# A delta-rule attention and slot router on one core: four edits to loads, solution weights, transposes and the shares of the inverse

## The chip, the cores and the metric

The kernel runs on 1 core of one Trainium2 chip. The metric is the device time of one execution in microseconds (us), lower is better. Eight executions of the kernel before the change took 373.21 to 382.68 us, with a median of 375.94 us. The profile in this document is of one execution that took 374.93 us.

The engines are named as the profile names them: PE is the matrix engine (PEld its weight loads), DVE the vector engine, ACT the scalar engine, POOL the general-purpose engine, SP the engine that here only issues DMAs. An ending q (SPq, ACTq) is the engine's instruction queue. Each engine runs its instructions strictly in the order in which they were written to it, and waits at an instruction whose inputs or whose target buffer are not ready, with everything behind it.

## The reference

Two blocks one after the other: a delta rule over 768 positions for 4 batches of 8 heads (head size 48), and a soft mixture of experts with 32 slots.

```python
def _attn_ref(q, k, v, beta):                 # (4, 8, 768, 48), beta (4, 8, 768)
    k_n = k / (np.linalg.norm(k, axis=-1, keepdims=True) + 1e-06)
    for t in range(S):
        kt, vt, bt = (k_n[:, :, t], v[:, :, t], beta[:, :, t, None])
        y[:, :, t] = np.einsum('bhd,bhde->bhe', q[:, :, t], state)
        v_old = np.einsum('bhde,bhd->bhe', state, kt)
        state = state + bt[:, :, :, None] * np.einsum('bhd,bhe->bhde', kt, vt - v_old)
...
def _moe_ref(x, phi, w1, w2):                 # x (3072, 384), 8 experts, F = 1024
    logits = x @ phi
    d = np.exp(logits - logits.max(0, keepdims=True))
    d /= d.sum(0, keepdims=True) + 1e-09
    slot_input = d.T @ x
...
        h = np.maximum(slot_input[e] @ w1[e], 0.0)
        slot_out[e] = h @ w2[e]
...
    c = np.exp(logits - logits.max(1, keepdims=True))
    c /= c.sum(1, keepdims=True) + 1e-09
    return (c @ slot_out).astype(np.float32)
```

## The kernel before

**Chunks and groups.** The 768 positions are cut into 24 chunks `x` of 32 positions. Four chunks make a group: group `n` is chunks 4n to 4n+3, and `c` is the place of a chunk in its group. A chunk covers all 4 batches and 8 heads at once. Within a chunk the recurrence is solved as a triangular system, so each chunk needs the inverse of a 32x32 triangular matrix for every batch and head. The inverses of a whole group are computed together on DVE, one group ahead.

**The recurrence of a chunk** (`chunk`, L392, called from the loop at L711) is a chain over four engines: `rest` (L411) multiplies the state with the keys on PE (L407) and DVE subtracts that from the scaled values into `R` (L414); `solve` (L417) multiplies `R` with the inverse `Tb` on PE (L421) and ACT copies the result to `U` (L424); `update` (L429) adds U times K to the state in `psS` on PE (L434) and ACT copies the new state to SBUF in two pieces (L441); the next chunk's `rest` needs that state. `read` and `outputs` (L426, L446) make the output `Y` beside it.

**The inverse of a group** (`invert`, L229): `spread` (L251) transposes the products of keys `GQ` into `lb` on DVE (L254) and takes the squared norms `ssq`; `root` (L263) is a logarithm and an exponential on ACT (L264, L265); `norms` (L267) is a row of ten DVE instructions that gives `gm`, scales `lb` (L281) and makes `nT`, by which POOL scales the values of that group (`scale_v`, L368, eight instructions at L371 for a chunk). Then come some 95 steps (L297, L302, L330) on DVE, and `back(0)` and `back(1)` transpose the two halves of the result into `TT` (L362). The first group's inverse runs by itself before the loop. For later groups `plan` (L610) deals the steps out over the chunks of the group before: `EL[c][p]` is a list for place p (0, 1, 2) of chunk c. `share` (L608) gives the share of the steps' weight for each place. `norms` stands at the head of `EL[0][0]`, `back(0)` in `EL[2][2]`, `back(1)` in `EL[3][2]`, and what is left of the steps goes to `EL[3][1]`.

**Weights of a chunk** (`weights`, L374) are made on POOL at the end of the chunk before: four instructions (L379) write `Ab`, and four copies (L385) put the inverse of the chunk from `TT` into `Tb`, each to the 32 partitions of one head, at place `h % 2` of a pair; the other place of the pair stays zero from a memset (L158). Both have three buffers, taken in turn.

**Preparation of later chunks** (`Prep`, L182): keys and queries are transposed on PE (L192), copied to `KQ` on ACT (L201, L208), and multiplied (`products`, L210: PE L221, ACT L225 to `GQ`). In the loop this runs eight chunks ahead (`later`, L704; the first chunks have a list of their own, L700, in which `q2 p2` of chunk 0 stands between `read` and `solve`).

**Router** (`route`, L473): each group's outputs are multiplied with `phi`, and softmax over tokens and slots is spread over the next group's chunks in lists `head`, `act`, `mid`, `vec`, `end`. In chunk c = 0 it ends with the logits (L481) and their copy `lT` (ACT L485); in c = 1 DVE begins with the maxima (L489), ahead of `EL[1][0]`; c = 2 ends with the two copies `dr` (ACT L563); sums of slots (PE L572) are added by DVE to `sacc` (L579 to L583) at c = 0.

**Order of one pass through the loop** (L721 to L771): loads are issued on SP; then `hook("head")`, `EL[c][0]`, `rest`, `read`, `scale_v(x + 2)`, `later(x, 0)`, `hook("act")`, `EL[c][1]`, from group 1 on at c = 3 `spread` of the group after next, `solve`, `turn`, `later(x, 1)`, `hook("mid")`, `hook("vec")`, `EL[c][2]`, `update`, `outputs`, `later(x, 2)`, `hook("end")`, `weights(x + 1)`, and at c = 3 `root` of the group after next. The order is written out by hand here; no scheduler changes it.

**Loads.** Keys, queries and values of a chunk are four DMAs of 48 KB each (L82, one for each h). Nearly all are issued from SP in the order of the program; K2 alone is issued from ACT. Eight completion counters are handed to the DMAs in turn, so an issue waits until the DMA eight before it has landed. Four buffers hold queries: Q4, Q5, Q6 share those of Q1, Q2, Q3.

**Experts** (from L784): the weights of the experts are loaded while the loop ends and after it, products on PE, and the output is written.

Of the kernel before, what the change touches and what calls it, by code (L numbers as in the profile page):

```python
# [8 lines left out]
F32 = mybir.dt.float32  # L9
AX = mybir.AxisListType  # L10
ALU = mybir.AluOpType
ACT = mybir.ActivationFunctionType
# [4 lines left out]
def kernel(  # L17
# [25 lines left out]
    nc = tc.nc  # L43
    P = 128
    B, H, S, D = q.shape
    C = 32
# [4 lines left out]
    U = B * G  # L51
# [15 lines left out]
    wk = att.enter_context(tc.tile_pool(name="wk", bufs=2))  # L67
# [18 lines left out]
    def load_k(cc, eng=nc.sync):  # L86
        load(k, Ks[cc % NK], cc, eng)

    def q_of(cc):

        return Qs[(cc - (LEAD // 2 <= cc < LEAD) * 3) % NQ]

    def load_q(cc, eng=nc.sync):
        load(q, q_of(cc), cc, eng)

    def load_v(cc, eng=nc.sync):
        Vt[cc] = io.tile([P, U, D], F32, name="V", tag="V", bufs=5)
        load(v, Vt[cc], cc, eng)
# [1 line left out]
    load_k(0)  # L100
    load_k(2, nc.scalar)
    load_k(1)
    load_k(3)

    one = cpool.tile([P, 1], F32, name="one")
    nc.vector.memset(one, 1.0)
    nc.scalar.preload_act_table_set("natural_log_exp_and_others")
    load_q(0)
    ident = cpool.tile([P, P], F32, name="ident")
    make_identity(nc, ident)  # L110
    for i in range(NK):
# [12 lines left out]
    own = cpool.tile([P, 2], F32, name="own")  # L124
# [13 lines left out]
            out=phi[g * D:(g + 1) * D],  # L138
            in_=moe_phi[g * 4 * D:(g + 1) * 4 * D].rearrange("(h d) s -> d h s", h=4))

    load_v(0, nc.sync)
    for i in range(4, 7):
        load_k(i)
        load_q(i)
    load_k(7)
# [6 lines left out]
        nc.vector.memset(t, 0.0)  # L152

    NT = 3
    Tb = [wk.tile([P, U, 2, C], F32, name=f"Tb{i}", bufs=1) for i in range(NT)]
    Ab = [wk.tile([P, U, 2, C], F32, name=f"Ab{i}", bufs=1) for i in range(NT)]
    for t in Tb + Ab:
        nc.vector.memset(t, 0.0)  # L158


# [19 lines left out]
    KQ, GQ, TT, nT = {}, {}, {}, {}  # L180
# [187 lines left out]
    def scale_v(cc):  # L368
        n, c = divmod(cc, GC)
        for u in range(U):  # L370
            nc.gpsimd.tensor_scalar(Vt[cc][:, u], Vt[cc][:, u], nT[n][:, c * U + u:c * U + u + 1],  # L371
                                    None, op0=ALU.mult)

    def weights(cc):  # L374
        n, c = divmod(cc, GC)
        for h in range(4):
            r = slice(C * h, C * h + C)

            nc.gpsimd.affine_select(  # L379
                out=Ab[cc % NT][r, :, h % 2, :].rearrange("p (b g) t -> p b g t", g=G),  # L380
                in_=GQ[n][r, c, :, :, 1, :], compare_op=ALU.is_gt, fill=0.0, base=0,
                pattern=[[0, B], [0, G], [1, C]], channel_multiplier=-1)
        for h in range(4):
            r = slice(C * h, C * h + C)
            nc.gpsimd.tensor_copy(Tb[cc % NT][r, :, h % 2, :], TT[n][r, c * U:(c + 1) * U, :])  # L385

# [3 lines left out]
    def chunk(cc, Yn):  # L392
        n, c = divmod(cc, GC)
        kq, K = KQ.pop(cc), Ks[cc % NK]
        at, T = ([t[cc % NT][64 * y:64 * y + 64].rearrange("p u x t -> p u (x t)")
                  for y in range(2)] for t in (Ab, Tb))
        half = [slice(64 * y, 64 * y + 64) for y in range(2)]
        old, new = St[cc % 2], St[1 - cc % 2]
        hs = [slice(C * h, C * h + C) for h in range(4)]
        st = {}  # L400

        ks, qs = (t[:, 0:U * D].rearrange("p (b g d) -> p b g d", g=G, d=D) for t in (psR, psY))

        def state(a, dst):
            for b in range(B):
                for h in range(4):
                    nc.tensor.matmul(dst[hs[h], b].rearrange("p g d -> p (g d)"),  # L407
                                     lhsT=kq[:, b, a, hs[h]], rhs=old[:, h, b, :],
                                     start=(b == 0), stop=False, skip_group_check=True)

        def rest():  # L411
            state(0, ks)
            R = st["R"] = wk.tile([P, U, D], F32, name="R", tag="R", bufs=1)
            nc.vector.tensor_tensor(R, Vt.pop(cc), ks.rearrange("p b g d -> p (b g) d"),  # L414
                                    op=ALU.subtract)

        def solve():  # L417
            pw = psR[:, 0:U * D].rearrange("p (u d) -> p u d", d=D)
            for u in range(U):
                for y in range(2):  # L420
                    nc.tensor.matmul(pw[half[y], u], lhsT=T[y][:, u], rhs=st["R"][half[y], u],  # L421
                                     start=(u == 0), stop=True, skip_group_check=True)
            st["U"] = wk.tile([P, U, D], F32, name="U", tag="U", bufs=1)
            nc.scalar.activation(st["U"], pw, ACT.Copy)  # L424

        def read():  # L426
            state(1, qs)

        def update():  # L429
            if cc == NCH - 1:  # L430
                return
            for b in range(B):
                for h in range(4):
                    nc.tensor.matmul(  # L434
                        psS[0:DP + D, h, b * GD:(b + 1) * GD],
                        lhsT=K[hs[h], b * G:(b + 1) * G].rearrange("p g d -> p (g d)")[:, 0:DP + D],
                        rhs=st["U"][hs[h], b * G:(b + 1) * G].rearrange("p g d -> p (g d)"),
                        start=(cc == 0 and b == 0), stop=True, skip_group_check=True)
            for g in range(G):
                r = slice(DP * g, DP * g + D)  # L440
                nc.scalar.activation(  # L441
                    new[r, :, :, g * D:(g + 1) * D],
                    psS[r, :, 0:B * GD].rearrange("p h (b g e) -> p h b g e", b=B, g=G)[:, :, :, g],
                    ACT.Copy)

        def outputs():  # L446
            for b in range(B):
                for g in range(G):
                    u = b * G + g
                    for y in range(2):  # L450
                        nc.tensor.matmul(qs[half[y], b, g], lhsT=at[y][:, u],  # L451
                                         rhs=st["U"][half[y], u],
                                         start=False, stop=True, skip_group_check=True)
            nc.scalar.activation(Yn[:, c, :, 0:GD], qs.rearrange("p b g d -> p b (g d)"),
                                 ACT.Copy)

        return rest, solve, read, update, outputs
# [137 lines left out]
    def drain(ls):  # L595
        for f in ls:
            f()
# [7 lines left out]


    PLACES = 3
    share = [(0.0, 0.14, 0.15), (0.10, 0.10, 0.10), (0.09, 0.09, 0.08), (0.10, 0.05, 0.0)]  # L608

    def plan(n):  # L610

        f = invert(n)
        at = [[[] for _ in range(PLACES)] for _ in range(GC)]
        at[0][0] += [f["norms"]]
        todo, done, total = f["steps"], 0.0, 0.0
        whole = sum(t[0] for t in todo)
        i = 0
        for c in range(GC):
            for p in range(PLACES):
                total += share[c][p] * whole  # L620
                while i < len(todo) and done + todo[i][0] / 2 < total:
                    done += todo[i][0]
                    at[c][p].append(todo[i][1])
                    i += 1
        at[2][2] += [lambda: f["back"](0)]
        at[3][1] += [t[1] for t in todo[i:]]
        at[3][2] += [lambda: f["back"](1)]
        return f, at
# [15 lines left out]
    f0["norms"]()  # L644
    pre[0].alone(1, 0)
    load_q(7)
    f0["clear"]()
    drain([t[1] for t in f0["steps"]])
    for i in range(2):
        f0["back"](i)  # L650
    pre[0].products(1, 2)
    for cc in range(4, 8):
        pre[cc] = Prep(cc)
        pre[cc].alone(0, 1)
        pre[cc].alone(1, 0)
        if cc > 4:
            pre[cc - 1].products()
    load_q(1)
    load_v(1)
    load_k(8)  # L660
    load_q(2)
    load_q(8)
    load_v(2)
    load_k(9)
    load_q(3)
    load_v(3)
    load_k(10)
    load_k(11)
    pre[7].products()
    pre[1].alone(1, 0)  # L670
    pre[1].products(1, 2)
    scale_v(0)
    weights(0)
    scale_v(1)

    empty = [[[]] * PLACES] * GC
    f, EL = plan(1)
    f["unit"]()
    f["spread"]()
    f["clear"]()  # L680
    f["root"]()
    routing, yT, late = [{}] * (GC + 1), {}, {}


# [19 lines left out]
    def later(x, place):  # L704
        if x in ahead:
            for w in ahead[x][place].split():
                step(int(w[1:]), w[0])
        else:
            step(x + LEAD + (place > 0), "ptu"[place])

    for x in range(NCH):  # L711
        n, c = divmod(x, GC)
# [4 lines left out]
        def hook(name):  # L717
            drain(late.get(name, []) if c == 0 else [])
            drain(routing[c].get(name, []))
# [20 lines left out]
        if x + 2 < NCH:  # L740
            scale_v(x + 2)
        later(x, 0)
        hook("act")
        drain(EL[c][1])
        if follow and x > GC:
# [2 lines left out]
        if x > 0:  # L748

            m, i = divmod(x - 1, GC)  # L750
# [15 lines left out]
        if c == GC - 1:  # L766
            EL = empty
            if follow:
                f, EL = follow
# [116 lines left out]
    for n in range(NG):  # L886
        for b in range(B):
            i = n * B + b
# [37 lines left out]
```

## Time and profile before

| | us |
|---|---|
| this execution | 374.93 |
| its span in the profile | 373.2 |
| first solve (L421, chunk 0) starts | 52.00 |
| R of chunk 4, 8, 12, 16, 20 starts | 94.08, 137.68, 184.03, 225.65, 264.55 |
| R of chunk 23 starts | 286.96 |
| last weights w2 landed | 346.8 |

The rows of the chunks are the starts of DVE's L414, one for each chunk. Between two of them lies the period of a chunk: 8 to 14 us in groups 1 to 4, where DVE also carries the inverse, 7 to 8 us in group 5, where it doesn't. After chunk 23 the chain goes through the last routing, the experts' first products at 306 us and the last loads of w2, and the output.

In a timeline row the columns are: start in us from the span's beginning, duration in us (of the whole run of equal instructions if there are several), engine, line, operation, output and inputs, shapes, number; in brackets the idle time of the engine ahead of it and what released it. In the group rows "x24 | 11.8, 492" means 24 instructions, 11.8 us of busy time, 492 ns for one. The engines' totals and the chain of waits are in the next part, as far as its steps rest on them.

### The profile page before, as it was taken

Reading aid. Unit: us, or ns where it says so; the run is one execution under the profiler, and the core shown is the slowest. Engines: PE = TensorE matmul, PEld = TensorE weight load, DVE = VectorE, ACT = ScalarE, POOL = GpSimd, SP = SyncE. Lnnn points to the kernel's source line nnn. Section 1 sums busy time; section 2 is a strip of 40 time slices with the busy share of each in tenths; the row PEclk is TensorE's granted clock in tenths of the full one; section 3 lists DMA queues with packets and bytes.
Section 4 is the critical chain, followed back from the end, with each engine's and each line's share of the span. In section 5 each row is a group of like instructions: output and inputs, shape, how many; then the busy total and the mean of one; then the engine's idle time right before and its main releaser. Section 6 shows DMA issues by size and latency. Waiting matters only on the chain.

```text
span 373.2 us, 16124 instructions
## 1 busy us (share of the span) xinstructions
PE 287.6 (77%) x6879; PEld 227.5 (61%) x6879; DVE 239.2 (64%) x801; ACT 145.3 (39%) x292; POOL 201.7 (54%) x434
## 2 busy tenths in 40 slices
PE   3667557887877989689788797689988779864784
PEld 2445446775766878578677676578877663311252
DVE  8399999785968979779696988889131220101043
ACT  2443124565334744356444652235455312000032
POOL 8460099993999379970899629994990000000000
PEclk9995659999589998679998998768999969999785
DMA  6555555554433344354101111105001997999058
GB/s 99 92 89 94 81 94 90 89 80 79 80 58 60 63 75 101 84 102 90 35 15 23 25 25 24 23 10 185 4 4 25 407 423 333 356 432 391 4 208 298
DMA packets 85031, 45.24 MB, mean 121 GB/s; under 512 B 79424, under 2 KB 82656, under 8 KB 83040
## 3 DMA queue, kind: packets, MB, share of 16 engines
q1 hardware_dynamic: 83296, 43.86, 43.7%
q8 instruction: 54, 0.88, 1.0%
q0 software_dynamic: 576, 0.15, 0.3%
q10 hardware_dynamic: 1088, 0.20, 0.3%
q14 instruction: 17, 0.14, 0.1%
HBM read 39.47 MB, written 4.72 MB: 118 GB/s over the span
## 4 chain that ended last, share of the span: by engine, by line
PE 47%; DVE 18%; SPq 11%; DMA 11%; ACT 7%; issue 4%; POOL 1%; DVEq 0%; ACTq 0%; POOLq 0%
SPq L82 10%; PE psR L421 7%; PE psS L434 6%; PE pt L572 6%; DMA w2t<-in_moe_w_dram 6%; PE psY L451 5%; PE pt L192 4%; PE pt L469 4%; PE pso L864 3%; DMA Q<-in_q_dram 3%; DVE R L414 3%; DVE tt L302 3%; ACT S L441 3%; DVE prL L297 2%; PE ph L840 2%
## 5 line engine op out<-in xcount | busy, mean ns | idle before, releaser
L371 POOL TENSOR_SCALAR V<-V,nT 128x48 f32<-128x48 f32 x192 | 91.2, 499 | 9.6 <-DMA Q<-in_q_dram 7.4
L385 POOL COPY Tb<-TT 32x256 f32<-32x256 f32 x96 | 43.1, 449 | 63.7 <-DVE TT L362 59.4
L421 PE MATMUL psR<-R,Tb 64*64 64x48 f32 x768 | 30.7, 234 | 32.1 <-DVE R L414 22.3
L379 POOL TENSOR_SCALAR_AFFINE_SELECT Ab<-GQ 32x256 f32<-32x256 f32 x96 | 48.2, 502 | 3.5
L421 PEld LDWEIGHTS psR<-R,Tb 64*64 64x64 f32 x768 | 28.1, 149 | 35.6 <-issue 25.9
L441 ACT ACTIVATE S<-psS 48x768 f32<-48x768 f32 x46 | 37.1, 806 | 27.1 <-PE psS L434 26.9
L221 PE MATMUL pt<-KQ 48*32 48x64 f32 (+1 forms) x1792 | 26.3, 237 | 12.6 <-ACT KQ L208 9.6
L424 ACT ACTIVATE U<-psR 128x384 f32<-128x384 f32 x24 | 11.8, 492 | 59.8 <-PE psR L421 47.4
L221 PEld LDWEIGHTS pt<-KQ 48*32 48x32 f32 x1792 | 21.3, 119 | 18.9 <-ACT KQ L208 11.1
L297 DVE TENSOR_TENSOR prL<-tt,nm 128x256 f32<-128x256 f32 (+7 forms) x96 | 29.7, 314 | 2.8
L297 DVE TENSOR_TENSOR prM<-tt,lb 128x16 f32<-128x16 f32 (+7 forms) x96 | 31.0, 323 | 0.0
L302 DVE TENSOR_TENSOR tt<-tt,prL 128x256 f32<-128x256 f32 (+7 forms) x96 | 30.9, 321 | 0.2
L302 DVE TENSOR_TENSOR nm<-nm,prM 128x16 f32<-128x16 f32 (+7 forms) x96 | 30.6, 319 | 0.0
L451 PE MATMUL psY<-U,Ab 64*64 64x48 f32 x768 | 30.1, 233 | 0.0
L302 DVE TENSOR_TENSOR tt<-tt,prE 128x30 f32<-128x30 f32 (+7 forms) x90 | 29.8, 331 | 0.0
L225 ACT ACTIVATE GQ<-pt 128x256 f32<-128x256 f32 (+1 forms) x56 | 16.7, 351 | 31.4 <-PE pt L221 31.4
L451 PEld LDWEIGHTS psY<-U,Ab 64*64 64x64 f32 x768 | 27.0, 147 | 2.7 <-issue 0.7
L297 DVE TENSOR_TENSOR prE<-tt,lb 128x30 f32<-128x30 f32 (+7 forms) x90 | 28.5, 317 | 0.0
L434 PE MATMUL psS<-U,K 32*112 32x96 f32 x736 | 27.7, 295 | 0.1
L434 PEld LDWEIGHTS psS<-U,K 32*112 32x112 f32 x736 | 23.6, 198 | 4.6 <-issue 2.0
L572 PE MATMUL pt<-Y,dr 64*64 64x97 f32 x384 | 22.5, 278 | 1.6 <-ACT dr L563 1.4
L407 PE MATMUL psR<-S,KQ 128*32 128x96 f32 x768 | 22.6, 263 | 0.7 <-ACT S L441 0.7
(133 smaller groups left out, 519.9 us busy)
## 6 DMA issues: line engine op xcount, KB each, us to landing
w2t<-in_moe_w_dram SPq DMA_DIRECT2D x8, 1536.0 KB, 19.2
w1t<-in_moe_w_dram SPq DMA_DIRECT2D x7, 1536.0 KB, 10.8
Q<-in_q_dram SPq DMA_DIRECT2D x96, 48.0 KB, 2.7
V<-in_v_dram SPq DMA_DIRECT2D x96, 48.0 KB, 2.6
out_dram<-ob SPq DMA_DIRECT2D x24, 192.0 KB, 2.4
K<-in_k_dram SPq DMA_DIRECT2D x92, 48.0 KB, 2.5
w1t<-in_moe_w_dram SPq DMA_DIRECT2D x3, 512.0 KB, 3.8
bb<-in_beta_dram POOLq DMA_DIRECT2D x16, 6.0 KB, 2.8
```

The source lines that it names most:

```text
L82: eng.dma_start(out=dst[C * h:C * h + C, :, 0:D], in_=src.rearrange("b (g h) s d -> h s (b g) d", h=4)[h, cc * C:(cc + 1) * C])
L221: nc.tensor.matmul(pg[g][rh, b], lhsT=kq[r, b, 0, rh], rhs=kq[r, b, a0:a1, rh], start=True, stop=True, skip_group_check=True)
L297: nc.vector.tensor_tensor(pr, a.broadcast_to([P] + shape), b.broadcast_to([P] + shape), op=ALU.mult)
L302: nc.vector.tensor_tensor(dst, dst, pr, op=op)
L371: nc.gpsimd.tensor_scalar(Vt[cc][:, u], Vt[cc][:, u], nT[n][:, c * U + u:c * U + u + 1], None, op0=ALU.mult)
L379: nc.gpsimd.affine_select(out=Ab[cc % NT][r, :, h % 2, :].rearrange("p (b g) t -> p b g t", g=G), in_=GQ[n][r, c, :, :, 1, :], compare_op= ...
L385: nc.gpsimd.tensor_copy(Tb[cc % NT][r, :, h % 2, :], TT[n][r, c * U:(c + 1) * U, :])
L421: nc.tensor.matmul(pw[half[y], u], lhsT=T[y][:, u], rhs=st["R"][half[y], u], start=(u == 0), stop=True, skip_group_check=True)
L434: nc.tensor.matmul(psS[0:DP + D, h, b * GD:(b + 1) * GD], lhsT=K[hs[h], b * G:(b + 1) * G].rearrange("p g d -> p (g d)")[:, 0:DP + D], rhs ...
L441: nc.scalar.activation(new[r, :, :, g * D:(g + 1) * D], psS[r, :, 0:B * GD].rearrange("p h (b g e) -> p h b g e", b=B, g=G)[:, :, :, g], A ...
L451: nc.tensor.matmul(qs[half[y], b, g], lhsT=at[y][:, u], rhs=st["U"][half[y], u], start=False, stop=True, skip_group_check=True)
L572: nc.tensor.matmul(pa[r], lhsT=st["dr"][r, c * B + b].rearrange("p x s -> p (x s)"), rhs=Yn[r, c, b, 0:GD + 1], start=(c == cs[0] and b == 0),
```

## The change

- **Loads.** K3 is issued from ACT behind K2, no longer from SP. On SP, K4, Q4 and V0 follow Q0 (before: V0, then K4, Q4). Later V1 goes ahead of Q1, and Q3 ahead of K9.
- **Solution weights.** The four POOL copies of `TT` into `Tb` become two ACT activations over all 128 partitions, which multiply with the column `x` of `own` (a 0/1 mask by partition), so that the zero places are written too. `Tb` has two buffers in place of three, and its memsets go.
- **Group 1's transposes.** `spread`, `root` and `norms` of group 1 move from ahead of the loop (and from ahead of R of chunk 0) to chunk 0, behind `rest`, `read` and `later(0, 0)`.
- **Shares.** The places of the inverse's steps: the first chunk of a group has 0.21 in place of 0.29, the second 0.31 in place of 0.30, the third 0.25 in place of 0.26, the last 0.23 in place of 0.15. By the built programs, R of the second chunk stands six inverse steps earlier in DVE's order, R of the third four, R of the last seven; between the maxima L489 and R of the second chunk there are 11 steps in place of 9.
- **Order of the values.** `scale_v(0)` is written earlier, but stands at the same place in POOL's order. PE's order is the same instruction by instruction.

```diff
     load_k(0)
     load_k(2, nc.scalar)
     load_k(1)
-    load_k(3)
+    load_k(3, nc.scalar)
...
     load_q(0)
+    load_k(4)
+    load_q(4)
+    load_v(0)
...
-    load_v(0, nc.sync)
-    for i in range(4, 7):
+    for i in range(5, 7):
         load_k(i)
         load_q(i)
     load_k(7)
...
     NT = 3
-    Tb = [wk.tile([P, U, 2, C], F32, name=f"Tb{i}", bufs=1) for i in range(NT)]
+    Tb = [wk.tile([P, U, 2, C], F32, name=f"Tb{i}", bufs=1) for i in range(2)]
     Ab = [wk.tile([P, U, 2, C], F32, name=f"Ab{i}", bufs=1) for i in range(NT)]
-    for t in Tb + Ab:
+    for t in Ab:
         nc.vector.memset(t, 0.0)
...
-        for h in range(4):
-            r = slice(C * h, C * h + C)
-            nc.gpsimd.tensor_copy(Tb[cc % NT][r, :, h % 2, :], TT[n][r, c * U:(c + 1) * U, :])
+        for x in range(2):
+            nc.scalar.activation(Tb[cc % 2][:, :, x, :], TT[n][:, c * U:(c + 1) * U, :],
+                                 ACT.Identity, scale=own[:, x:x + 1])
...
-        at, T = ([t[cc % NT][64 * y:64 * y + 64].rearrange("p u x t -> p u (x t)")
+        at, T = ([t[cc % len(t)][64 * y:64 * y + 64].rearrange("p u x t -> p u (x t)")
...
-    share = [(0.0, 0.14, 0.15), (0.10, 0.10, 0.10), (0.09, 0.09, 0.08), (0.10, 0.05, 0.0)]
+    share = [(0.0, 0.10, 0.11), (0.11, 0.10, 0.10), (0.09, 0.08, 0.08), (0.11, 0.12, 0.0)]
...
-        at[0][0] += [f["norms"]]
+        if n > 1:
+            at[0][0] += [f["norms"]]
...
     load_q(7)
+    load_v(1)
     f0["clear"]()
...
     load_q(1)
-    load_v(1)
     load_k(8)
     load_q(2)
     load_q(8)
     load_v(2)
+    load_q(3)
     load_k(9)
-    load_q(3)
     load_v(3)
...
     f["unit"]()
-    f["spread"]()
     f["clear"]()
-    f["root"]()
...
         later(x, 0)
+        if x == 0:
+            f["spread"]()
+            f["root"]()
+            f["norms"]()
         hook("act")
         drain(EL[c][1])
```

## The prediction, made before the changed kernel ran

> **What bounds the kernel now.** I read the totals first, then the chain of waits, then the timelines of DVE, PE, ACT and POOL around each row of R (L414), because the shares of a whole span mix stages with different limits.
>
> ```profile
> PE 287.6 (77%) x6879; PEld 227.5 (61%) x6879; DVE 239.2 (64%) x801; ACT 145.3 (39%) x292; POOL 201.7 (54%) x434
> ```
>
> ```profile
> PE 47%; DVE 18%; SPq 11%; DMA 11%; ACT 7%; issue 4%; POOL 1%; DVEq 0%; ACTq 0%; POOLq 0%
> ```
>
> No engine is full and the chain changes hands. POOL, which the change relieves, holds 1% of it; ACT, which gets more to do, 7%.
>
> The start, from the timeline:
>
> ```profile
> 7.36 1.08 PE L192 MATMUL psY<-ident,K 128*128 128x128 f32 x4 [0.64 <-DMA K<-in_k_dram]
> ...
> 45.44 1.82 DVE L254 STREAM_TRANSPOSE lb<-GQ 128x1024 f32<-128x1024 f32 x1
> 45.65 1.71 POOL L385 COPY Tb<-TT 32x256 f32<-32x256 f32 x4 [17.96 <-DVE TT L362]
> ...
> 48.55 0.89 PE L221 MATMUL pt<-KQ 48*32 48x32 f32 x64 [5.14 <-ACT KQ L208]
> ...
> 52.00 1.94 PE L421 MATMUL psR<-R,Tb 64*64 64x48 f32 x32 [2.56 <-DVE prE L297]
> ...
> 67.01 0.30 PE L192 MATMUL pt<-ident,Q 128*128 128x128 f32 x1 [0.47 <-DMA Q<-in_q_dram]
> ```
>
> PE waits for K1 at 7.36. The first inverse is done at 45.59, yet the first solve starts at 52.00, because group 1's transposes and norms lie ahead of it on DVE and, through the root, on ACT. At 67.01 PE waits for Q9: SP has issued one load of 0.49 us after the other until there.
>
> In the loop DVE decides part of each group. Two stretches, group 3 and then group 4, hold the same instructions with POOL's Tb copies beside them and without:
>
> ```profile
> 193.73 0.47 DVE L302 TENSOR_TENSOR tt<-tt,prE 128x120 f32<-128x120 f32 x1
> 194.13 0.55 DVE L302 TENSOR_TENSOR nm<-nm,prM 128x160 f32<-128x160 f32 x1
> ...
> 235.37 0.29 DVE L302 TENSOR_TENSOR tt<-tt,prE 128x120 f32<-128x120 f32 x1
> 235.58 0.34 DVE L302 TENSOR_TENSOR nm<-nm,prM 128x160 f32<-128x160 f32 x1
> ```
>
> The end of group 3:
>
> ```profile
> 220.25 0.19 DVE L260 TENSOR_SCALAR ssq<-lb 128x32 f32<-128x32 f32 x1
> 220.35 1.07 DVE L362 STREAM_TRANSPOSE TT<-tt 128x512 f32<-128x512 f32 x1
> 222.18 0.32 DVE L583 SCALAR_TENSOR_TENSOR sacc<-sacc,al,pt 128x97 f32<-128x97 f32 x1 [0.76 <-PE pt L572]
> 222.41 0.34 DVE L272 RECIPROCAL rn<-nrm 128x32 f32<-128x32 f32 x1
> ...
> 225.65 0.51 DVE L414 TENSOR_TENSOR R<-V,psR 128x384 f32<-128x384 f32 x1
> ```
>
> The root ran on ACT at 221.82 to 222.31, before which ACT waited for nothing of TT; the norms follow, and R of chunk 16 behind them.
>
> **Loads.** K3's four issues leave SP: 4 x 0.49 = 1.94 us for all behind them. But two queues take the eight counters twice as fast. By the built program K1's issues now wait for K0's landings and K3's for K2's. K0's and K2's last landed at 5.50 and 5.66, and K1's last was issued at 4.85, so it moves 0.65 later; PE had no slack for K1 (0.64 us idle). K3 ends on ACT at 5.66 + 0.45, and the table load (1.28) behind it at 7.4, where the first KQ copy ran at 6.76: the same 0.6, in parallel. So the first inverse starts 0.6 late, and Q0 is issued at 6.0 in place of 7.32: SP gains 1.3. Bounds: 0 (all given back) to 1.94. DMA engines were 0.93 busy at 160 GB/s while both queues issued (2 to 3 us) and 0.73 at 119 with one (8 to 9 us).
>
> The Trainium skill (DMA: Bandwidth & Descriptors, "Issuing engines are not separate DMA queues") says that DMAs issued from several engines share the same 16 DMA engines and save only issuing time. By that rule the sum would hold the 1.94 of SP's time and no delay of K1, 0.6 less than mine; the rows with two queues, near full at 0.93, agree with the first half of it, and the delay is one that the page does not speak of.
>
> **First group.** TT at 45.59 + 0.6 = 46.2; two activations for Tb (0.75, below), the KQ copy of q2 (0.6), its products (0.95): first solve at about 48.5, 3.5 earlier. Next late are two others. DVE: spread, root, norms took 45.44 to 51.42, 6 us; behind R(0), and the root behind ACT's GQ of p2 at 49, they end at 52.6; then the steps before R(1), 9.7 us, lose six (1.65) and Tb's contention (0.8): R(1) at about 60 in place of 61.87. SP: Q9 lands 1.3 earlier, and PE's order puts its transposes ahead of update(1). So 1.3 stays, with 1.9 as the upper bound. DVE idled 2.19 ahead of R(2) and 0.75 ahead of R(3), where PE's chain decides; the 1.3 is kept. V0 and V1 are needed from 21 and 48 on and land long before.
>
> **Tb on ACT.** POOL loses 96 x 449 ns = 43.1 us. For ACT no row has this shape: GQ 128x256 takes 381 ns without a scale pointer, dr 128x512 689 ns with one where KQ 128x512 takes 593. So 381 + 96 = 477 for one, and in a pair the second starts about 0.1 before the first ends: 0.75 until ACT is free, 0.85 until Tb is there. Bounds 0.66 (the GQ pair) to 1.27 (the dr pair). 24 pairs are 18 us on ACT. Most lie in gaps of 1 to 5 us ahead of U. Behind a pair stand GQ, dT and U of the next chunk, with room, except in two places. (a) Behind dr in chunks 18 and 22: dr ended at 257.95 and 287.25, solves started 258.36 and 287.66; with Tb between, 0.45 late each, +0.9. (b) At a group's end, where the root follows Tb on ACT and Tb waits for TT.
>
> **Contention.** Against the shortest of each form, DVE instructions that lie mostly beside L385 are 10.4 us longer in all. On the chain lie those between the maxima L489 and R of the second chunk in groups 1 to 3 (0.87, 0.88, 0.86) and 0.3 elsewhere; the others fall before waits for PE. So -2.9; bounds -1 to -6. The masks L379, 13.9 in all and 3.9 on the chain, stay on POOL, but with a quarter less work it does them right after `outputs`, mostly beside DVE's waits: I take half, -1.9, bounds 0 to -3.9.
>
> **Shares.** In chunk c = 0 the relieved DVE arrives earlier at L489, but lT came at 192.60 and 234.44 against 192.64 and 234.47 for L489, and group 1 idled 3.2 there: PE's chain to the logits decides, gain 0. Behind L489 two more steps stand ahead of R: 2.74 us for R behind L489 in group 4, 9 steps, so +0.5 in each of four groups, +2.0. c = 1 and c = 2 are even (R(c2) to R(c3): 7.5 us of DVE before, 7.7 after). Behind R of the last chunk stand seven steps more, 1.65 us, ahead of spread and TT.
>
> **Group ends, (b).** Group 0: TT is early, the root waits for the pair only, +0.75. Group 1: TT ended 132.66, now 134.3; pair and root (0.5) to 135.6 in place of 134.61, +1.0. Group 2: TT's 1.65 fits into 2.64 idle, the pair costs +0.5. Group 3: 221.44 + 1.65 = 223.1, pair 223.9, root 224.4, norms then in place of 222.41: +2.0. Sum +4.3; bounds +2 (a pair at 0.66, TT's delay hidden) to +6.5 (a pair at 1.27).
>
> **Sum.** -1.3 - 2.9 - 1.9 + 2.0 + 4.3 + 0.9 = +1.1 us on the execution's 374.93: 376.0. That execution lies 1.0 under the median of 375.94, so against the median 377.0. The tail is carried along one to one: at 317 us the products of the first four experts, which free the buffers of later loads, and the loads issued at 287 to 291 end together.
>
> **Rivals.**
> 1. *POOL was the brake.* All contention on the chain goes, Tb's and the masks', and half of what I left off it: -2.9 - 3.9 - 3.7. With +7.2 for the group ends, steps and dr, and -1.9 at the start: -5.2, about 370.7. For it: the pairs of rows above. Against: the rows where DVE waits for PE (L502, L536, lT) right behind most Tb copies.
> 2. *The root behind Tb decides (slower).* ACT's order makes DVE's norms wait for TT plus a pair at every group end. At 1.27 a pair this is +6.5, dr +1.9, steps +2.0, nothing from the masks, -1.0 from Tb's contention and -0.5 from the start: +8.9, about 384.8. It decides, over 1%, once the rises pass the savings by 3.8. For it: ACT's order. Against: 2.64 and 1.84 us of idle DVE at two of four ends.
> 3. *The start gives nothing.* K1 later and Q9 no earlier: +1.3, 378.3, within 1% by itself.
>
> **How the numbers follow.** Within 1%, 3.8 us, this kernel's executions cannot be told from no change. The forecast, with rival 3 inside it, has 0.65; rival 1 has 0.22, of which 0.20 lies under 372.2; rival 2 has 0.13. The bounds of the terms lie below my values by 0.6, 3.1, 2.0 and 2.3 (start, Tb, masks, ends), together 4.4 if independent, and above them by 1.3, 1.9, 1.9, 2.2 and 1.0 (dr), together 3.8: 372.6 to 380.8. Below, it is carried to 371.2, to leave about half of rival 1 out, as the upper end leaves out most of rival 2. Faster 0.20, same 0.64, slower 0.16 (rival 2 and the top of the forecast).
>
> **What would show it.** First solve near 48.5 and R(1) near 60; PE still idle ahead of Q9, at about 65.7; PE at K1 near 8.0; Tb pairs near 0.85 us on ACT; R behind L489 after about 2.8 us in groups 1 to 4; a longer wait ahead of L489; root starts behind Tb, norms' start to R unchanged at 3.1 to 3.5; R(23) at about 288. The prediction is wrong if R(4) gains over 2 us, if group 3's period does not grow by its end, or if TT is never late for the root.

## The result and the profile after

The changed kernel takes 382.05 us (median of 11, 378.25 to 387.59) where the kernel before, run beside it, takes 377.0 (32 runs, 373.21 to 383.58): 1.0146 times as long, 95% interval 1.0108 to 1.0184, or 5.5 us more. (A ratio takes only the executions of a kernel that lie within 1.5% of its fastest, a median takes all of them, so the two can differ.) The forecast was +1.1 us on the execution. The profiled execution took 380.23 us, its span 378.5 (before 374.93 and 373.2).

The page of the kernel after, totals and chain of waits:

```profile
PE 289.1 (76%) x6879; PEld 227.9 (60%) x6879; DVE 222.8 (59%) x798; ACT 164.7 (44%) x340; POOL 154.8 (41%) x338
```

```profile
PE 44%; DVE 16%; DMA 14%; SPq 10%; ACT 10%; issue 4%; DVEq 0%; ACTq 0%
```

POOL fell by 46.9 us, DVE's busy time by 16.4 with the same inverse, ACT rose by 19.4. The relief that was to be had is there. In the chain, though, transfers grew from 11% to 14% and ACT from 7% to 10%.

The start, from the timeline of the kernel after:

```profile
9.12 1.08 PE L194 MATMUL psY<-ident,K 128*128 128x128 f32 x4 [1.88 <-DMA K<-in_k_dram]
...
47.29 0.91 ACT L386 ACTIVATE Tb<-TT,own 128x256 f32<-128x256 f32 x2 [8.59 <-DVE TT L364]
...
47.56 1.93 DVE L256 STREAM_TRANSPOSE lb<-GQ 128x1024 f32<-128x1024 f32 x1
...
48.73 0.89 PE L223 MATMUL pt<-KQ 48*32 48x32 f32 x64 [6.41 <-ACT KQ L210]
...
49.55 1.94 PE L423 MATMUL psR<-R,Tb 64*64 64x48 f32 x32
...
67.46 0.45 PE L194 MATMUL pt<-ident,Q 128*128 128x128 f32 x1 [3.46 <-DMA Q<-in_q_dram]
```

K1's transposes stand 1.76 us later than before and everything up to the first inverse 1.6. The moved transposes more than make up for it: the first solve at 49.55 (52.00 before), R of chunk 0 at 47.11 (51.34). But Q9 comes at 67.46, in place of 67.01, and PE has run out of work 3.46 us earlier. What follows that wait shows in the rows of the matmuls behind it (after, then before; the second column is the duration of the same 32 matmuls):

```profile
69.12 1.82 PE L436 MATMUL psS<-U,K 32*112 32x96 f32 x32
70.87 1.94 PE L453 MATMUL psY<-U,Ab 64*64 64x48 f32 x32
...
73.86 1.51 PE L409 MATMUL psR<-S,KQ 128*32 128x96 f32 x32
```

```profile
67.89 1.04 PE L434 MATMUL psS<-U,K 32*112 32x96 f32 x32
68.86 1.14 PE L451 MATMUL psY<-U,Ab 64*64 64x48 f32 x32
...
70.76 0.87 PE L407 MATMUL psR<-S,KQ 128*32 128x96 f32 x32
```

Each takes 1.7 times as long. The windows say why. After a window's two times and its length stand the busy times of PE, PEld, DVE, ACT and POOL, each with its number of instructions, then the granted clock, the DMA share and GB/s. After, then before:

```profile
63.00:67.40 4.40, 1.00 (x5) 0.58 (x3) 3.76 (x17) 0.97 (x2) 4.37 (x7) 0.50 0.51 87
67.40:70.00 2.60, 2.54 (x27) 2.24 (x27) 0.00 (x0) 1.20 (x2) 2.42 (x6) 0.50 0.60 96
70.00:73.00 3.00, 3.00 (x77) 2.74 (x78) 0.00 (x0) 1.72 (x3) 1.15 (x3) 0.50 0.64 103
```

```profile
67.40:70.00 2.60, 2.60 (x78) 2.29 (x82) 2.19 (x5) 1.99 (x4) 2.40 (x5) 1.00 0.49 83
70.00:73.00 3.00, 2.45 (x128) 2.06 (x128) 1.12 (x3) 1.75 (x4) 3.00 (x8) 1.00 0.45 75
```

The clock stands at 0.50 from 62.9 to 76.6 us. It dropped 1.1 us before the wait for Q9 began, after a stretch (59.5 to 62.9) in which PE was half busy, with one gap of 1.71 us; the kernel before has a gap of 1.43 us at the same place, and its clock stayed at 1.00: there the gap lay across two of the windows of the last section (60.4 to 63.8 and 63.8 to 67.2). The idle time from 64.00 to 67.46 then kept the clock down, and it rose only after PE had been full for some 7 us. R of chunk 2 comes at 75.59 (71.85 before): of the 4.2 us won at R of chunk 0, 0.8 are left at R of chunk 1, and at R of chunk 2 they have turned into 3.7 lost.

Over the whole span the two executions differ by 5.3 us. 4.9 of them stand at R of chunk 4; groups 1 and 2 are then 2.3 and 3.0 us shorter than before, group 3 is 3.7 longer, groups 4 and 5 are within 0.4, and 2.4 us arise behind R of chunk 23, where the two programs are the same. The time at half clock moves the same way (after, against before: 3.4 and 6.8 us in groups 1 and 2, against 10.2 and 13.7; 15.8 in group 3, against 3.4), so one pair of executions can't tell what a later group has won or lost by the edits.

The end of group 3 (DVE and ACT, after):

```profile
223.28 1.10 DVE L364 STREAM_TRANSPOSE TT<-tt 128x512 f32<-128x512 f32 x1
...
224.41 0.91 ACT L386 ACTIVATE Tb<-TT,own 128x256 f32<-128x256 f32 x2 [1.34 <-DVE TT L364]
225.22 0.21 ACT L266 ACTIVATE nrm<-ssq 128x32 f32<-128x32 f32 x1
...
225.73 0.35 DVE L274 RECIPROCAL rn<-nrm 128x32 f32<-128x32 f32 x1 [1.26 <-ACT nrm L267]
...
228.91 0.50 DVE L416 TENSOR_TENSOR R<-V,psR 128x384 f32<-128x384 f32 x1
```

Here DVE waits 1.26 us for the root, ACT's root stands behind the pair of Tb, and the pair has waited 1.34 for TT: the chain that the prediction described.

### The profile page after: what moved, and what is told of

Same layout as the page of the kernel before. It is cut to its first block, busy times and chain, and to the rows that moved or that the text cites. A ratio compares the mean times of both kernels' runs of the same rounds, so it can differ in the third digit from the quotient of the medians.

```text
span 378.5 us, 16079 instructions
## 1 busy us (share of the span) xinstructions
PE 289.1 (76%) x6879; PEld 227.9 (60%) x6879; DVE 222.8 (59%) x798; ACT 164.7 (44%) x340; POOL 154.8 (41%) x338
## 4 chain that ended last, share of the span: by engine, by line
PE 44%; DVE 16%; DMA 14%; SPq 10%; ACT 10%; issue 4%; DVEq 0%; ACTq 0%
SPq L82 9%; PE psR L423 6%; PE psS L436 6%; DMA w2t<-in_moe_w_dram 6%; PE pt L574 5%; PE psY L453 4%; PE pt L194 4%; DMA Q<-in_q_dram 4%; PE pso L869 3%; ACT S L443 3%; PE pt L471 3%; PE pt L223 2%; DVE prL L299 2%; DVE tt L304 2%; DVE R L416 2%
## 5 line engine op out<-in xcount | busy, mean ns | idle before, releaser
L373 POOL TENSOR_SCALAR V<-V,nT 128x48 f32<-128x48 f32 x192 | 89.6, 491 | 35.5 <-DMA V<-in_v_dram 18.7
L381 POOL TENSOR_SCALAR_AFFINE_SELECT Ab<-GQ 32x256 f32<-32x256 f32 x96 | 45.6, 475 | 30.3 <-PE psY L453 26.1
L423 PEld LDWEIGHTS psR<-R,Tb 64*64 64x64 f32 x768 | 27.0, 145 | 34.4 <-issue 24.6
L304 DVE TENSOR_TENSOR nm<-nm,prM 128x16 f32<-128x16 f32 (+7 forms) x96 | 29.5, 307 | 0.0
L299 DVE TENSOR_TENSOR prM<-tt,lb 128x16 f32<-128x16 f32 (+7 forms) x96 | 29.2, 304 | 0.1
L304 DVE TENSOR_TENSOR tt<-tt,prL 128x256 f32<-128x256 f32 (+7 forms) x96 | 29.1, 303 | 0.2
L436 PE MATMUL psS<-U,K 32*112 32x96 f32 x736 | 28.4, 300 | 0.1
L436 PEld LDWEIGHTS psS<-U,K 32*112 32x112 f32 x736 | 24.2, 203 | 4.6 <-issue 1.7
L386 ACT ACTIVATE Tb<-TT,own 128x256 f32<-128x256 f32 x48 | 21.6, 502 | 10.3 <-DVE TT L364 10.3
L299 DVE TENSOR_TENSOR prE<-tt,lb 128x30 f32<-128x30 f32 (+7 forms) x90 | 24.2, 269 | 0.0
L251 POOL MEMSET nm<- 128x256 f32 x6 | 1.9, 312 | 53.9 <-DVE tt L304 49.3
L304 DVE TENSOR_TENSOR tt<-tt,prE 128x30 f32<-128x30 f32 (+7 forms) x90 | 23.9, 265 | 0.0
```

The source lines that it names most:

```text
L299: nc.vector.tensor_tensor(pr, a.broadcast_to([P] + shape), b.broadcast_to([P] + shape), op=ALU.mult)
L304: nc.vector.tensor_tensor(dst, dst, pr, op=op)
L381: nc.gpsimd.affine_select(out=Ab[cc % NT][r, :, h % 2, :].rearrange("p (b g) t -> p b g t", g=G), in_=GQ[n][r, c, :, :, 1, :], compare_op= ...
L386: nc.scalar.activation(Tb[cc % 2][:, :, x, :], TT[n][:, c * U:(c + 1) * U, :], ACT.Identity, scale=own[:, x:x + 1])
L436: nc.tensor.matmul(psS[0:DP + D, h, b * GD:(b + 1) * GD], lhsT=K[hs[h], b * G:(b + 1) * G].rearrange("p g d -> p (g d)")[:, 0:DP + D], rhs ...
```

## The experiments

Each kernel was timed beside the kernel before, whose median lay between 375.9 and 379.6 us; ratios are to that, and differences between two kernels are differences of their ratios, times 377 us. Executions of one kernel are 0.4 to 4.1% apart (the last section has a likely cause), so the intervals matter. "The wall" below is the place where PE waits for Q9.

**One part undone.** Four kernels, each the diff of the change backwards in one part. By the medians of all executions they stand at 1.007, 1.018, 1.014 and 1.010 times the kernel before, and the changed kernel at 1.013: none differs clearly from it.

```diff
-    load_k(3, nc.scalar)
+    load_k(3)
...
```

> The changed kernel with the old loads (K3 on SP again, the old order of K4, Q4, V0, V1, Q3); all else as changed. Against the changed kernel's 382.05 us. Theory 'the wait for Q9' (the start's gain is stopped where PE waits for Q9 at 67 us, and PE's idling there halves its clock): the first inverse is done 1.6 us earlier (45.7 in place of 47.3), Q9 lands where it did, R of chunk 2 stays near 75.6, so 382 within 1 us. Theory 'late loads' (K1 behind K0's landings is carried to the end): 380.4, R of chunk 2 at 74.

380.66 us, 1.0151 (1.0041 to 1.0261): no gain. The first solve came at 48.05, 1.5 earlier, and PE stood the longer at the wall, as the first theory had it, but Q9 itself came 1.07 us later than in the changed kernel, which that theory did not have (timeline of this kernel):

```profile
68.53 0.45 PE L192 MATMUL pt<-ident,Q 128*128 128x128 f32 x1 [6.96 <-DMA Q<-in_q_dram]
```

```diff
-        for x in range(2):
-            nc.scalar.activation(Tb[cc % 2][:, :, x, :], ...
+        for h in range(4):
+            nc.gpsimd.tensor_copy(Tb[cc % NT][r, :, h % 2, :], ...
```

> The changed kernel with Tb made by POOL's four copies again (three buffers); all else as changed. Theory 'the root behind Tb' (ACT's pair of 0.91 us and TT ahead of the root delay the norms at the ends of groups 0, 1 and 3): 377 to 379, and no idle DVE of 1 to 2.3 us ahead of the norms. Theory 'POOL was the brake': 385 to 387, with groups 1 and 2 longer by about 2.5 us each. Theory 'the wait for Q9': chunk 1 stays long (R of chunk 2 near 75), and the whole moves by less than 2 us either way.

384.6, 1.0152 (0.9993 to 1.0312), too wide to decide. In the trace the last chunk of group 0 is 12.58 us again (14.00 changed, 12.59 before), and R of chunk 2 still late at 74.01.

```diff
+    f["spread"]()
     f["clear"]()
+    f["root"]()
...
-        if x == 0:
-            f["spread"]()
...
```

> The changed kernel with group 1's transposes, root and norms ahead of the first R again; all else as changed. Theory 'the wait for Q9': the first solve is later by 3 to 4 us (about 53), PE is busy up to the wait for Q9, its clock stays at 1.00 there, and R of chunk 2 comes at 72 to 73 in place of 75.6: 378.5 to 380. Theory 'the moved transposes help': R of chunk 2 later than now by 1 to 3 us, 383 to 385.

383.08, 1.0223 (1.012 to 1.0327): no gain, a miss for the theory of the wait, taken alone. PE indeed had no wait for Q9 and ran at 1.00 behind it, but R of chunk 0 came at 53.02 and R of chunk 2 at 74.24: the late loads and the early transposes, together, put the first chunk 1.7 us behind the kernel before, and PE was at half clock from 33 to 67 us in this execution.

```diff
-    share = [(0.0, 0.10, 0.11), (0.11, 0.10, 0.10), (0.09, 0.08, 0.08), (0.11, 0.12, 0.0)]
+    share = [(0.0, 0.14, 0.15), (0.10, 0.10, 0.10), (0.09, 0.09, 0.08), (0.10, 0.05, 0.0)]
```

> The changed kernel with the old shares; all else as changed. Theory 'the shares cost' (two more steps behind the maxima in each of four groups, +2.0, and TT 1.65 us later at the group ends): 379 to 380, TT's second half 1.6 us earlier. Theory 'they lie beside waits': 382 within 0.8.

381.65, 1.0113 (0.988 to 1.0347): not decided here. Group 3's last chunk was 1.06 us shorter (10.47 for 11.53).

**The wall, the root, the clock.** The loads and the moved transposes both undone:

> The changed kernel with both the old loads and group 1's transposes, root and norms ahead of the first R: what is left of the change is Tb on ACT, the even shares and V0 scaled earlier. Theory 'the start' (late K1, and the gain of the first solve lost at the wait for Q9): R of chunk 2 back at 72 as before, the rest as in the changed kernel, 378 to 379. Theory 'the group ends' (Tb and the shares hold all of the loss): 381 to 382.

381.15, 1.0092 (1.0045 to 1.0139). Without the changed start 0.92% remain, 3.5 us (+/- 1.8); the start holds the other 0.54%, 2.0 us (+/- 2.3).

Q9 alone moved up in SP's order:

```diff
-    queries = {0: (), 1: (9, 10, 11), 2: (12, 13), 3: (14,), 4: (15, 16)}
+    queries = {0: (9,), 1: (10, 11), 2: (12, 13), 3: (14,), 4: (15, 16)}
```

> The changed kernel with Q9 issued ahead of V4 and K13 (12 issues of 0.49 us earlier in SP's order); all else as changed. Theory 'the wait for Q9': PE's wait of 3.46 us ahead of Q9 goes, the clock stays at 1.00 there, R of chunk 2 comes at 71 to 72.5 in place of 75.6: 378 to 379. Theory 'something else holds chunk 1': R of chunk 2 within 1 us of 75.6, 382.

By the program and the trace Q9 moves ahead of two loads, eight issues, not twelve: it is issued at 58.51 in place of 62.79. 374.51, 0.9876 (0.9807 to 0.9945): 2.7% off the changed kernel, 10.2 us (+/- 3.0), the largest effect of all parts. R of chunk 2 at 68.70, 6.9 earlier. Timeline and windows of this kernel at the same place:

```profile
63.87 0.30 PE L194 MATMUL pt<-ident,Q 128*128 128x128 f32 x1 [0.40 <-DMA Q<-in_q_dram]
...
64.75 1.04 PE L436 MATMUL psS<-U,K 32*112 32x96 f32 x32
```

```profile
63.00:67.40 4.40, 4.00 (x138) 3.47 (x137) 3.57 (x16) 3.45 (x6) 1.07 (x3) 1.00 0.49 86
```

The wait is 0.40, the clock 1.00, and L436 back at 1.04.

That this is no luck of one execution shows over all traces of kernels with the moved transposes. In the six with Q9 late (the changed kernel among them) the clock was at half for 3.4 to 13.7 us between 60 and 78 us, and R of chunk 4 came at 95.7 to 99.0. In the eight with Q9 early, this one and those that follow, it was at half for 3.4 us in one and never in the other seven, and R of chunk 4 came at 91.0 to 92.7.

The root ahead of the pair at the group ends:

```diff
         hook("end")
-        if x + 1 < NCH:
-            weights(x + 1)
         if c == GC - 1:
...
                 f["root"]()
+        if x + 1 < NCH:
+            weights(x + 1)
```

> The changed kernel with the root of the next group ahead of the pair of Tb copies on ACT at each group's end; all else as changed. Theory 'the root behind Tb': DVE's waits of 2.25, 1.0 and 1.26 us ahead of the norms go, the last chunks of groups 0, 1 and 3 are 1.3, 0.8 and 1.5 us shorter: 378 to 379. Theory 'DVE's own work decides there': less than 1 us gained, 381 to 382.

378.8, 0.9984 (0.9936 to 1.0032): 1.6% off the changed kernel, 6.1 us (+/- 2.3). Its trace shows the place (ACT's root ahead of TT, DVE's norms right behind):

```profile
224.29 0.23 ACT L266 ACTIVATE nrm<-ssq 128x32 f32<-128x32 f32 x1 [0.30 <-DVE ssq L262]
...
225.31 0.91 ACT L386 ACTIVATE Tb<-TT,own 128x256 f32<-128x256 f32 x2 [0.53 <-DVE TT L364]
```

The last chunks of groups 0, 1 and 3 shrank from 14.00, 11.54 and 11.53 to 13.01, 11.13 and 10.76, together 2.2 us, where 3.6 were expected. That is shown, and with Q9 early the same edit took 2.0 us off the same three chunks; that the remainder up to 6 belongs to the root is not shown, and with Q9 early the time fell by only 0.24% (+/- 1.0). The edit also puts POOL's masks `Ab` of the next chunk behind the memset of `clear`.

The kernel before, with TensorE kept busy where it waits:

```diff
+            nc.tensor.matmul(psS[:, 0, 256:384], lhsT=ident, rhs=ident,
+                             start=first and i == 0, stop=True, skip_group_check=True)
...
+        warm(fill, x == 0)
         solve()
```

> The kernel before, with matmuls of the identity into unused columns of the state's bank put on TensorE where it waits for R (5 to 10 ahead of the solve in chunks 0, 4, 5, 6, 8, 9, 10, 12, 13, 14, 16, 17 and 18, about 0.21 us each) and 20 ahead of the products that wait for the first inverse; nothing reads them. Theory 'the clock gate' (a window of 3.41 us in which PE is less than half busy puts its clock at 0.5): granted clock above 0.93 in place of 0.87 and 8 to 15 us faster, 361 to 369 against 376 to 378. Theory 'the slow stretches lie beside waits for DVE': clock up, time within 2 us of before. Theory 'filling delays the solves': slower by 2 to 5 us.

372.44, 0.9837 (0.9774 to 0.9899): 6.1 us faster with more work, clock 0.914 (0.869 before). These matmuls changed what the state's bank holds, so the run is read for its time alone; the later ones have a PSUM tile of their own. The gain was below the 8 expected: in this execution PE waited 3.5 us for Q9 too, the stretch behind it ran at 0.50, and chunk 1 took 14.4 us in a kernel that had shown 9.97.

**Combinations.** Q9 early in the kernel before:

> The kernel before with Q9 alone issued ahead of V4 and K13. Theory 'one wall for both': the wait for Q9 bounded the kernel before as well (its first two periods, 10.5 and 10.0, are the lucky case; with PE idle there they are 14), so it gains 1 to 5 us, 372 to 376 against the same runs of before at 377 to 379. Theory 'the wall bounds only the changed kernel': within 1 us of before.

377.3, 0.9928 (0.9875 to 0.9982): 2.7 us (+/- 2.0). The wall was there before; the change made it dearer, by 10.2 less 2.7, 7.5 us (+/- 3.6). With Q9 early in both kernels, 0.9876 against 0.9928, the change is worth -2.0 us (+/- 3.3): the loss of 5.5 is gone.

Q9 early and the old loads:

> The changed kernel with Q9 ahead of V4 and K13 and the old loads. With the wait for Q9 gone, the 1.6 us by which the new loads delay the first inverse should now reach the end: first solve at 47.4 in place of 49, 1 to 2 us faster than the changed kernel with Q9 alone moved (374.5), 372.5 to 373.5. If the new loads are no loss once Q9 is early (Q4, V1 ahead), the same 374.5 or more.

375.96, 0.9943 (0.9898 to 0.9988), against 0.9876 with the new loads: 0.67% (+/- 0.83) the other way. The 1.6 us by which the first inverse comes late do not reach the end; expectation missed.

Q9 early and the root ahead:

> The changed kernel with Q9 ahead of V4 and K13 and the root ahead of the pair of Tb copies at the group ends. If the two losses lie in different stages and add: about 9 and 3 to 4 us off the changed kernel's 382, 369 to 372. If they share one cause: 374 as with Q9 alone.

373.2, 0.9852 (0.9781 to 0.9923): as with Q9 alone, within the noise, and by its median less than the sum.

The same, with matmuls of the identity ahead of the solves:

```diff
+            t = pt([P, P])
+            for i in range(count):
+                nc.tensor.matmul(t, lhsT=ident, rhs=ident, start=True, stop=True,
+                                 skip_group_check=True)
```

> As the last, with matmuls of the identity into the rotating tile of PSUM where TensorE waits for R: 5 to 14 of about 0.21 us ahead of the solve in chunks 4, 5, 6, 8, 9, 10, 12, 13, 14, 16, 17 and 18, and 11 ahead of the products behind the first inverse; nothing reads them. Theory 'the clock gate': granted clock above 0.92, 5 to 8 us faster than without them, 362 to 366. Theory 'the slow stretches lie beside waits': the same time within 2 us, 369 to 372.

365.37, 0.9669 (0.9597 to 0.9742): 7.8 us by the medians, 6.9 (+/- 3.8) by the ratios, clock 0.926. The idle PE time ahead of R had looked free; it cost the clock of the work behind it.

**What was still open.** The wait for Q9, kept, with 8 such matmuls ahead of it:

> The changed kernel with 8 matmuls of the identity (0.21 us each at full clock) ahead of the transposes of K9 and Q9 in chunk 1; nothing reads them, and Q9 comes as late as it did. Theory 'the clock is the loss' : the stretch behind Q9 runs at 1.00 sooner, R of chunk 2 at 72 to 74 in place of 75.6, 378 to 380.5 against 382. Theory 'the wait is the loss': R of chunk 2 stays at 75 to 76, 382.

379.89, 1.0054 (1.0009 to 1.0099): 3.5 us (+/- 2.2) off the changed kernel with Q9 as late as ever. Windows of this kernel:

```profile
63.00:67.40 4.40, 2.94 (x39) 2.65 (x33) 3.57 (x16) 1.24 (x3) 4.40 (x7) 1.00 0.54 86
67.40:70.00 2.60, 2.11 (x35) 1.98 (x39) 0.00 (x0) 1.09 (x2) 2.36 (x7) 0.79 0.63 94
70.00:73.00 3.00, 3.00 (x108) 2.74 (x104) 0.00 (x0) 2.10 (x3) 1.01 (x2) 0.61 0.43 75
```

The half clock shrinks from 13.7 us to 3.4. R of chunk 2 comes at 74.20, 1.4 us earlier, although Q9 came 0.43 later, and just short of the 72 to 74 of the first theory. So part of the loss is the clock, part the wait itself; with Q9 early and the moved transposes, R of chunk 2 comes at 67.9 to 70.7.

The old first group (loads and transposes), Q9 early, root ahead:

> The kernel with Q9 early and the root ahead of Tb, with the old loads and group 1's transposes ahead of the first R: against the same with the changed first group (373.2). Theory 'the start is a gain behind the wall': R of chunk 2 at 72 in place of 70.1, slower by 1.5 to 3 us, 375 to 376. Theory 'the start is a loss of its own': 371 to 372.

378.95 (372.56 to 380.91, a wide spread, so that median and ratio differ), 0.9972 (0.9908 to 1.0035) against 0.9852: the changed start is worth 1.2% (+/- 0.95), some 4.5 us, once Q9 is out of its way.

The old shares in the same kernel:

> The kernel with Q9 early and the root ahead of Tb, with the old shares. By the prediction's terms the even shares cost 2.0 behind the maxima and up to 1.65 at a group's end: 370 to 372 against 373.2, the last chunk of group 3 about 1 us shorter. If the steps lie beside waits for PE: 373 within 0.8.

372.03, 0.9892 (0.9845 to 0.9939): no difference that shows.

More filling, in the tail too:

```diff
+                if q == 1 and t == 0 and j > 1:
+                    w = bank("tr", [P, P])
+                    for i in range(12):
+                        nc.tensor.matmul(w, lhsT=ident, rhs=ident, ...
```

> The kernel with Q9 early, the root ahead of Tb and the matmuls of the identity ahead of the solves (365.4), with 6 more in chunk 19 and 12 each ahead of the last two products that wait for the second expert weights. Theory 'the clock decides the tail too': 2 to 3 us faster, 362 to 363.5, the products behind the last wait in 6.3 us in place of 7.9. Theory 'weights and outputs on the queues decide there': 365 within 1.

359.8 (359.11 to 360.56), 0.9567 (0.9524 to 0.9609), clock 0.947: 5.6 us by the medians, 3.8 (+/- 3.2) by the ratios, where 2 to 3 were expected. The products behind the last weights, with the 24 matmuls of the identity ahead of them (timeline of this kernel, then of the kernel before; the trace has up to two records for a matmul):

```profile
328.66 4.96 PE L883 MATMUL tr<-ident 128*128 128x128 f32 x42
333.54 5.35 PE L885 MATMUL pso<-w2t,hT 128*32 128x384 f32 x60
```

```profile
346.82 7.18 PE L864 MATMUL pso<-w2t,hT 128*32 128x384 f32 x58 [2.72 <-DMA w2t<-in_moe_w_dram]
```

Its executions lie within 0.4%, where the kernel before spreads over 2.8%. In it the two remaining parts could be measured. Tb back on POOL:

> The fastest kernel so far (359.8) with Tb made by POOL's four copies again. By the prediction's terms POOL's copies cost 4.8 us of contention, and there is no pair on ACT (dr, 0.9): 363 to 364. Theory 'POOL is the brake once TensorE is fast': 365 to 370, with solves waiting for Tb in the third and fourth chunks of a group. Theory 'the copies lie beside waits': 359 to 361.

363.92, 0.9692 (0.9653 to 0.9731): Tb on ACT is worth 1.25% (+/- 0.6), 4.7 us (4.1 by the medians). Not all of that is shown to be contention: of the 3.7 us between the two profiled executions 2.3 stand at R of chunk 23, and 1.4 arise behind it, where Tb has no part and the clock was at half for 24.4 us against 17.3. DVE's inverse steps show the contention, group rows with POOL's copies and without:

```profile
L304 DVE TENSOR_TENSOR tt<-tt,prE 128x30 f32<-128x30 f32 (+7 forms) x90 | 28.1, 312 | 0.0
```

```profile
L304 DVE TENSOR_TENSOR tt<-tt,prE 128x30 f32<-128x30 f32 (+7 forms) x90 | 23.4, 260 | 0.0
```

Over all 564 step instructions 177.6 us against 166.3. The old shares:

> The fastest kernel so far (359.8) with the old shares. By the prediction's terms the even shares cost 0.5 behind the maxima in each of four groups and up to 1 us at the end of group 3: 357 to 358. Theory 'they lie beside waits': 359.3 to 360.3. Theory 'even shares help': 361 to 363.

358.75 (356.82 to 359.02), 0.9541 (0.9505 to 0.9577): the fastest version, 4.6% under the kernel before. The medians put the even shares at 1.05 us of cost; the intervals of the two ratios overlap, so the size stays open.

## Why the prediction was wrong

**The step that failed is the first term, the start at -1.3.** It said "SP gains 1.3", with Q0 issued at 6.0. Q0 went out at 7.31, as before (7.32). With two queues taking turns at the counters, each of K1's issues waited for a landing of K0 (issued at 3.23, 4.14, 4.98 and 6.03; before 3.51, 3.86, 4.36, 4.85), and Q0 behind them waited again: SP's waits for landings of K are 3.3 us in all, 0.8 before. The four issues taken from SP were paid in waits, as rival 3 had it: from SP's first issue to Q9's, the time beyond 0.49 us an issue grew from 8.0 to 11.0 us, more than the 1.94 saved. K1 moved 1.76 us, not 0.65.

The next sentence, "So 1.3 stays", fails with it, and worse. It took Q9 as the next late thing and moved it 1.3 earlier; Q9 came 0.45 later. Everything won on the way there (2.45 us at the first solve, where 3.5 were forecast) became idle PE time at the wall, and around that idle time the clock was at half for 10 us of PE work. (In the profile of the kernel before the clock stayed at full there, which was luck: in its run with added matmuls it was at half for 10.2 us at the same place.) The prediction knew the wait, in its own first rows, and read it as a limit that takes a gain away. It did not ask what an idle TensorE costs afterwards: none of its terms holds the granted clock. Against a forecast of -1.3, undoing the start gained 2.0 us (+/- 2.3), which leaves 0 possible but not -1.3; taking the wall away gained 10.2 (+/- 3.0), 7.5 more than it did in the kernel before.

**The terms for the rest fit, within wide intervals.** Their sum was +2.4; the kernel without the changed start measures +3.5 (+/- 1.8). One by one they are less sure:
- Contention and dr, -4.8 and +0.9: Tb on ACT measures -4.7 (+/- 2.2) where the clock is kept up, in a kernel without the term of the group ends and with a part that may be clock. The masks' -1.9 was not measured by itself. Rival 1 (POOL the brake) needed 10.5 us of relief, and rival 2's +8.9 would have needed the savings to fail.
- Group ends, +4.3 (0.75, 1.0, 0.5, 2.0): the last chunks of groups 0 to 3 went from 12.59, 10.25, 11.50 and 9.38 to 14.00, 11.54, 11.52 and 11.53, so +1.4, +1.3, 0 and +2.15, together 4.9, at full clock wherever PE had work, in one pair of executions; putting the root first took 2.2 us back. The mechanism is the one named, TT, then the pair, then the root. A pair takes 0.91 us, where 0.85 was expected.
- Shares, +2.0: about 1, not resolved. From the start of the maxima to R it took 2.95, 2.47, 2.54 and 2.78 us in groups 1 to 4 (2.8 was forecast; 3.03, 3.36, 3.24 and 2.74 before). In groups 1 to 3 shorter steps more than paid for the two added ones, and in group 4, where none of POOL's copies lay beside them before, they cost 0.04 in place of 0.5.
- dr: one of the two places showed it (chunk 23: R to solve 1.13 us, 0.70 before), chunk 19 did not.
- The tail, "carried along one to one": not in this pair. From R of chunk 23 to the end it took 88.6 us, 86.3 before; over all the traces of kernels without added matmuls in the tail it lies between 85.9 and 90.1.

**Its stated signs.** First solve 49.55 (48.5), R of chunk 1 at 61.03 (60), K1 at 9.12 (8.0), PE idle ahead of Q9 until 67.46 (65.7), norms to R 3.2 to 3.7 (3.1 to 3.5), DVE's wait ahead of the maxima longer (1.1 to 3.5 us, 0 to 3.2 before), R of chunk 23 at 289.89 (288). None of its three refuting signs came (R of chunk 4 lost 4.9 us, group 3 grew by its end, TT was late for the root): they asked whether the gain was too great or a group's end failed to grow, and none could have shown a start that loses.

## What to carry to other kernels

A gain ahead of a fixed arrival is not only lost there: look whether the engine that now idles loses its clock, and move the arrival (here one tile's loads, eight issues up) before anything in front of it. On a kernel whose TensorE is 70 to 80% busy in bursts, read the granted clock by stage, and try cheap matmuls in the waits: 5 to 14 of them ahead of each late solve took 7.8 us off. And in such a kernel small parts are best measured after that, when executions agree.

## What the hardware showed

**The clock changes on a grid.** In the windows of 20 profiled executions every change of the granted clock up to 340 us, 6 to 28 an execution, lies within 0.02 us of a grid of 3.4135 us whose offset differs from one execution to the next (0.90, 1.47, 2.37, 3.09...). The Trainium skill (TensorE: Matmul & The Clock Gate, "What's actually happening") gives a free-running window of 3413 ns, which agrees. Sorted by the share of such a window in which PE was busy (60 to 330 us; at full clock the number that ended in a drop, at half clock in a rise):

```
PE busy in window   at 1.00: windows, drops   at 0.50: windows, rises
under 0.4                  78    78                   5     0
0.4 to 0.5                 48    44                   3     0
0.5 to 0.6                 64    23                   2     0
0.6 to 0.7                 66    13                  20     0
0.7 to 0.8                161     0                   9     0
0.8 to 0.9                176     0                  40    10
over 0.9                  671     0                 218   153
```

A drop comes after a window that is less than about half busy, a rise only after one that is nearly full. The same page ("HAM oscillation — how this bites in real kernels") puts the rule as no idle gap over about 3.4 us; here 136 of the 158 drops came without one, and gaps of 2 to 3 us were enough where a window held one of them. The stretches at half clock behind them lasted 3.4 us (70 of them), 6.8 us (52) or 10.2 us (36). Waits of much the same length for Q9, 3.46, 3.51 and 3.15 us, stood beside 13.7, 10.2 and 6.8 us at half clock (the changed kernel, the kernel before with added matmuls, Tb back on POOL). Since the offset is another in each execution, a gap can cost such a stretch in one execution and less or nothing in the next. That fits the spread of the kernel before (10 us) and its absence in the filled kernel (1.5 us), but it is not shown to be the cause: in the changed kernel a longer execution goes with a lower mean clock (correlation -0.86 over twelve executions), in the kernel before only weakly (-0.28 to -0.56 in five sets). The profiled execution of before had met the wall without a drop.

**Two queues, fewer issues, no gain.** With K2 and K3 on ACT's queue, SP's first eight issues took 5.53 us, where the first twelve took 6.46 with K2 alone there.
